# Keys of attention blocks 8 to 23 turned by transposing transfers instead of by PE

## The chip, the cores and the metric

One core of a Trainium2 chip. The time is device microseconds of one execution of the whole program. The kernel before took 1919.92 us (median of two runs, 1918.02 and 1921.83).

## The reference

A chunked attention feeds a mixture of experts. q, k and v are fp32 of shape (4, 8, 768, 64): batch, heads, positions, features.

```python
scale = 1.0 / np.sqrt(D)
for c in range(S // 32):                    # chunks of 32 queries
    k_ctx = k[:, :, max(0, 32*c - 16) : min(S, 32*c + 32 + 8)]
    k_full = concat(mem_k, k_ctx)           # 8 memory keys and a window of up to 56
    scores = scale * q_c @ k_full.T
    a = exp(scores - scores.max(-1)); a /= a.sum(-1) + 1e-9
    out_c = a @ v_full
x = out as (3072, 512)
P = exp(x @ w_gate - max); 8 times: rows of P, then columns, are brought to a common sum
out = sum over 8 experts of P[:, e] * (relu(x @ w1[e]) @ w2[e])     # w1 512x1024, w2 1024x512
```

What the change touches is `q_c @ k_full.T`. To make it on PE, the 64 features must lie on the partitions, so queries and keys are turned (transposed) first. All this is fp32.

## The kernel before, in words

**Two kinds of work.** Attention goes by 24 blocks of 128 queries (6 per batch, each 4 chunks of 32). Four blocks make a unit of 512 tokens; there are 6 units. The expert part goes through 48 steps, one for an expert and a unit, in split fp16 products by a Strassen scheme (`hidden`, `output`: matmuls px, py, pz and yx, yy, yz at line 1598, plain products yp at line 2126 for expert 0). Expert 0 can do a unit only when its four attention blocks are done, so attention blocks and expert 0 are woven together through the first 290 us or so; after that come experts 1 to 7, which need no more attention.

**What sets the order.** Nothing is issued as it is written. Every step is a `Task` with an engine, a cost, a due time and the steps that it waits for; `Plan.run` plays the program through with these costs and writes each engine's instructions in the order that comes out. It is a fixed list per engine, and each engine works through its list in order. Transfers are tasks of SP, with `cost` times 0.5 us for the issuing and `dma` us for the transfer. Where the plan foresees a gap of more than 0.4 us on PE, `Plan.pad` fills it with matmuls on the identity (`warm`, line 427), `int((at - now - 0.1) * 0.8 / 0.11)` of them, whose results nobody uses. Buffers are rings (`Ring`, `buf`): a task that writes a slot waits for the last users of that slot. A block's due time is `needed(n)`: 50 us for four blocks, from 88 us at block 8 on.

**A block.** `load_block` (lines 831 to 851) loads 128 query rows (q) and 128 key rows (k, beginning 16 positions ahead of the block), both as rows of 8 heads x 64 features, 256 bytes a head. `load_extra` (766 to 827) loads for the four blocks of a unit the 24 keys after each block's 128 and 8 memory keys into one tile kx of 4 x 32 rows; PE turns kx (line 806, tx) and ACT copies it to kxT (line 813). `transposed` (995 to 1044) lets PE turn q (line 1006, tq) and k (line 1010, tk), four 128x128 fp32 transposes each, and ACT copies out of PSUM: qT with the factor 1/8 (line 1034), and into kC the 56-key windows of three chunks (1014), the first 32 keys of the fourth (1020), its next 24 from kxT (1023) and, at the first block of a batch, the 8 memory keys (1027). kC (features of a head pair, 4 pairs, 4 chunks, 64 keys) has one buffer in before. `scores` (1047) multiplies (line 1069, sp), DVE takes the maximum and subtracts it, ACT takes the Exp (line 1108). `values` turns the softmax (ta, 1127), multiplies it with v (xp, 1137), DVE divides (1155), and PE turns the result back (xt, 1178). `load_values` brings v in 8 to 10 transfers a block (line 921). `logits` does the gate's products (lp, lq).

**Queues.** SP issues nearly all transfers: q, k, kx, v; the expert weights w1 and w2 (`load`, lines 549 and 551; the m tiles are a first look for the maxima); stores and loads of the partial sums (akeep, lines 2150, 2013, 1847); stores of a unit's split operands (xkeep, 1256) and of later units' raw ones (gkeep, xs). POOL does the sums for the Strassen blocks of weights (602) and of tokens (1290 to 1314), in order, and copies of memory values (913).

## Time and profile before

| | |
|---|---|
| median of the runs | 1919.92 us |
| profiled execution, span | 1917.9 us |
| PE busy | 1903.2 us (99%), clock 1.000 |
| LDWEIGHTS busy (PEld) | 1641.0 us (86%) |
| DVE, ACT, POOL busy | 1436.4, 1033.6, 524.4 us |
| DMA | 254.82 MB, 133 GB/s over the span |
| 0 to 40 us | PE 36.04 us busy, DMA share 0.85 |
| 40 to 80 us | PE 38.17 us busy, DMA share 0.66 |
| 80 to 120 us | PE 38.54 us busy, DMA share 0.81 |
| 160 to 200 us | PE 39.00 us busy, DMA share 0.84 |
| 240 to 280 us | PE 40.00 us busy, DMA share 0.58 |
| 400 to 500 us | PE 98.65 us busy, DMA share 0.37 |

The program does not wait before or after the span for anything that the profile shows, so its time and the run's are taken as one. PE is busy nearly always. The DMA engines and SP's queue are much busier in the first 280 us, where attention is loaded and expert 0 stores its sums, than later. A query of the trace gives for a line its instructions, their time and what their engine waited for; a view by windows gives the busy time of each engine in a stretch.

### The profile page before, as it was taken

The page shows a single profiled execution, that of the slowest core. Times are in us where ns is not written, and L with a number is a line of the kernel's source. Part 1 is how long each engine was busy: PE and PEld are TensorE (multiplying, and loading weights), DVE is VectorE, ACT ScalarE, POOL GpSimd, SP SyncE. Part 2 cuts the span into 40 slices and gives each one's busy share as a digit, 9 for nine tenths or more (in the row PEclk, how much of TensorE's full clock was granted, in tenths as well). Part 3 has the DMA queues.
Part 4 walks back from the last instruction along what each step waited for, and adds up shares of the span by engine and source line. Part 5 has one row for each costly group of instructions (what it writes and reads, how often), then busy time and mean ns, then how long its engine had stood idle before and what let it go on. Part 6 is the DMA issues. An engine that isn't in the chain of part 4 may idle for free.

```text
span 1917.9 us, 47295 instructions
## 1 busy us (share of the span) xinstructions
PE 1903.2 (99%) x19616; PEld 1641.0 (86%) x19616; DVE 1436.4 (75%) x2396; ACT 1033.6 (54%) x2019; POOL 524.4 (27%) x549
## 2 busy tenths in 40 slices
PE   9999999999999999999999999999999999999999
PEld 7777676688888888888888888888888888888888
DVE  6776569778679866898668875898678885786565
ACT  4765565556456545646445554655555554564453
POOL 1220001544224221432124231342124232332112
PEclk9999999999999999999999999999999999999999
DMA  8678753453235342265214533245313732322321
GB/s 198 174 194 209 171 172 116 129 204 125 83 110 172 127 148 85 78 197 185 92 63 149 197 105 127 78 160 176 138 45 105 242 122 94 100 83 84 127 83 67
DMA packets 246791, 254.82 MB, mean 133 GB/s; under 512 B 113264, under 2 KB 180272, under 8 KB 242224
## 3 DMA queue, kind: packets, MB, share of 16 engines
q1 hardware_dynamic: 244452, 251.21, 41.2%
q8 instruction: 153, 2.51, 0.6%
q10 hardware_dynamic: 2124, 0.59, 0.2%
q14 instruction: 62, 0.51, 0.1%
HBM read 187.84 MB, written 63.44 MB: 131 GB/s over the span
## 4 chain that ended last, share of the span: by engine, by line
PE 96%; DMA 2%; DVE 1%; ACT 0%; issue 0%; SPq 0%; ACTq 0%; DVEq 0%
PE px L1598 26%; PE yx L1598 23%; PE pz L1598 13%; PE yz L1598 11%; PE py L1598 6%; PE yp L2126 6%; PE yy L1598 6%; DMA q<-in_q_dram 1%; PE xp L1137 1%; PE sp L1069 1%; PE pp L2045 1%; PE tq L1006 1%; PE tk L1010 0%; PE ta L1127 0%; PE xt L1178 0%; DVE w L521 0%
## 5 line engine op out<-in xcount | busy, mean ns | idle before, releaser
L1598 PEld LDWEIGHTS <-w 128*128 128x128 f16 x7896 | 771.4, 98 | 91.9 <-issue 0.6
L1598 PEld LDWEIGHTS <-h 128*128 128x128 f16 x7056 | 690.4, 98 | 81.4 <-issue 1.5
L1598 PE MATMUL px<-x,w 128*128 128x256 f16 x4512 | 549.1, 273 | 0.0
L1931 POOL TENSOR_TENSOR acc<-acc,y 128x256 f32<-128x256 f32 x252 | 267.5, 1068 | 862.1 <-ACT y L1906 842.7
L1598 PE MATMUL yx<-w,h 128*128 128x256 f16 x4032 | 467.5, 273 | 1.3 <-DVE acc L1941 1.3
L1657 ACT ACTIVATE q<-px 128x256 f32<-128x256 f32 x376 | 142.8, 381 | 294.2 <-PE px L1598 289.5
L1598 PE MATMUL pz<-x,w 128*128 128x256 f16 x2256 | 278.2, 273 | 0.0
L1598 PE MATMUL yz<-w,h 128*128 128x256 f16 x2016 | 233.8, 273 | 0.0
L1826 DVE TENSOR_TENSOR h<-ss,h 128x1024 f16<-128x1024 f32 x160 | 215.0, 1346 | 4.0 <-ACT h L1802 3.5
L1777 ACT ACTIVATE h<-c 128x768 f16<-128x768 f32 x168 | 140.8, 838 | 106.4 <-DVE c L1667 106.4
L1802 ACT CAST h<-ss 128x1024 f16<-128x1024 f32 x168 | 174.1, 1039 | 20.4 <-DVE ss L1766 19.6
L1766 DVE SCALAR_TENSOR_TENSOR ss<-c,ss 128x256 f32<-128x256 f32 x336 | 168.3, 501 | 8.2
L1810 DVE SCALAR_TENSOR_TENSOR h<-c,h 128x768 f16<-128x768 f32 x168 | 165.3, 984 | 9.2 <-ACT h L1777 9.1
L1667 DVE SCALAR_TENSOR_TENSOR c<-px,q 128x256 f32<-128x256 f32 x188 | 78.0, 422 | 103.2 <-PE px L1598 94.9
L1906 ACT ACTIVATE y<-yx,pscale 128x256 f32<-128x256 f32 x168 | 79.4, 473 | 114.8 <-PE yx L1598 110.6
L1598 PE MATMUL py<-x,w 128*128 128x256 f16 x1128 | 139.2, 273 | 0.0
L2126 PE MATMUL yp<-w,h 128*128 128x512 f16 x576 | 132.0, 379 | 0.0
L1667 DVE SCALAR_TENSOR_TENSOR c<-py,q 128x256 f32<-128x256 f32 x188 | 78.5, 422 | 60.2 <-PE py L1598 56.7
L1766 DVE SCALAR_TENSOR_TENSOR ss<-c,h 128x512 f32<-128x512 f32 x168 | 120.8, 719 | 3.1 <-ACT h L1754 3.0
L1598 PE MATMUL yy<-w,h 128*128 128x256 f16 x1008 | 116.9, 273 | 0.0
L2126 PEld LDWEIGHTS <-h 128*128 128x128 f16 x576 | 56.0, 98 | 57.9
L513 ACT ACTIVATE w<-ws,sw 128x1024 f16<-128x1024 f32 (+1 forms) x64 | 69.3, 1089 | 65.5 <-POOL ws L602 65.5
(158 smaller groups left out, 1773.0 us busy)
## 6 DMA issues: line engine op xcount, KB each, us to landing
x<-xkeep SPq DMA_DIRECT2D x28, 1792.0 KB
akeep<-acc SPq DMA_DIRECT2D x168, 256.0 KB
acc<-akeep SPq DMA_DIRECT2D x168, 256.0 KB
w1f<-in_moe_w_dram SPq DMA_DIRECT2D x72, 256.0 KB
w2f<-in_moe_w_dram SPq DMA_DIRECT2D x32, 512.0 KB
w1fm<-in_moe_w_dram SPq DMA_DIRECT2D x56, 256.0 KB
w2fm<-in_moe_w_dram SPq DMA_DIRECT2D x28, 512.0 KB
xkeep<-x SPq DMA_DIRECT2D x6, 1792.0 KB
```

The costliest lines, as they stand in the source:

```text
L513: lambda: nc.scalar.activation(dst(0), src(), AF.Copy, scale=s),
L1598: nc.tensor.matmul(dst.t, a, b, start=(not more and n == 0), stop=(n == end), skip_group_check=more,)
L1657: lambda: nc.scalar.activation(t.t, src.t, AF.Copy, scale=DOWN),
L1667: lambda: nc.vector.scalar_tensor_tensor(c.t[:, o], src.t, DOWN, q.t, op0=ALU.mult, op1=ALU.add),
L1766: lambda: nc.vector.scalar_tensor_tensor(dst(), src(), 0.0, other(), op0=ALU.max, op1=op),
L1777: lambda: nc.scalar.activation(h.t[:, 0, 0:3], c.t, AF.Relu),
L1802: lambda: nc.scalar.copy(h.t[:, 0, 3:7], ss.t),
L1810: lambda: nc.vector.scalar_tensor_tensor(h.t[:, 1, 0:3].rearrange("p a n -> p (a n)"), c.t.rearrange("p a n -> p (a n)"), 0.0, h.t[:, 0, 0 ...
L1826: lambda: spare.tensor_tensor(h.t[:, 1, 3:7], ss.t, h.t[:, 0, 3:7], op=ALU.subtract),
L1906: (lambda: nc.scalar.activation(t.t, src.t, AF.Copy, scale=f))
L1931: lambda: nc.gpsimd.tensor_tensor(acc.t[:, cols], acc.t[:, cols], q.t, op=ALU.add),
L2126: nc.tensor.matmul(py.t, hf.t[:, hl, where[fh], o : o + P], room(fp, WIDE * wl + DM * fh, WIDE * wl + DM * (fh + 1)), start=(fp == 0 and i ...
```

## The change

For blocks 8 to 23 (`DT = 2 * BU = 8`), PE no longer turns the keys, and ACT no longer copies them into kC:

- POOL copies each key tile into a tile of half words: of each fp32 element the two 16-bit halves go to two planes, 128 rows x 2 x 512 (`plane`, one copy a block). The same for kx of units 2 to 5.
- SP writes the two planes to DRAM, 256 KB a tile (`kplane`, `eplane`).
- SP reads them back by transposing transfers on 2-byte elements (`turn_rows`) straight into kC seen as half words. The planes' rows of one key lie next to each other in DRAM, so that the two halves of a turned element land next to each other. A block has three of 112 rows (56 keys), one of 64 and one of 48 rows (`go_own`, `go_next`), and at the first two blocks after a batch has begun four of 16 rows for the memory keys (`go_memory`). At the first of them here POOL copies the memory keys from the other buffer instead.
- kC gets a second buffer (kC2). Until block 8 its space holds kx and kxT, which were tiles of their own.
- Keys of these blocks are loaded 50 us ahead of need, where it was 25; blocks are loaded one block earlier in program order. Their query transposes stay on PE (`turn_q`).
- For all blocks the factor 1/8 moves from the copy of qT into the scale of the Exp.

The order of all engines comes out of the plan anew. By count of instructions: PE 64 key transposes and 16 of kx fewer, 210 warm matmuls more (378, not 168); ACT 55 instructions fewer; POOL 20 plane copies and one copy of memory keys more; SP 20 plane writes and 96 transposing transfers more.

```diff
@@ -12,6 +12,7 @@
...
 I32 = mybir.dt.int32
+U16 = mybir.dt.uint16
 AF = mybir.ActivationFunctionType
...
@@ -333,6 +334,8 @@
...
     gkeep = [dram.tile([P, KT * GT], F32, name=f"gkeep_{g}") for g in range(2 * NU)]
+    kplane = [dram.tile([2 * QB, H * D], U16, name=f"kplane_{n}") for n in range(NBLK)]
+    eplane = [dram.tile([2 * QB, H * D], U16, name=f"eplane_{u}") for u in range(NU)]
     akeep = [dram.tile([P, DM], F32, name=f"akeep_{T}") for T in range(NT)]
...
@@ -740,9 +743,14 @@
...
+    DT = 2 * BU
     state = {}
     extra = {}
+    extra_users = []
     kC_tile = att.tile([P, HP, CB, KW], F32, name="kC")
+    kC2_tile = att.tile([P, HP, CB, KW], F32, name="kC2")
+    kx_tile = kC2_tile.rearrange("p i c k -> p (i c k)")[:, 0 : H * D].rearrange("p (h d) -> p h d", h=H)
+    kxT_tile = kC2_tile.rearrange("p i c k -> p (i c k)")[:, H * D :].rearrange("p (i t) -> p i t", i=HP)
...
@@ -766,9 +774,13 @@
-        kx = buf("kx", att, [P, H, D], F32, f"kx_{u}")
-        kxT = buf("kxT", att, [P, HP, P], F32, f"kxT_{u}")
-        tx = bank("att", [P, HP, P], f"tx_{u}")
+        if u * BU >= DT:
+            kx = buf("k", att, [P, H, D], F32, f"kx_{u}")
+        else:
+            kx = rings["kx"].take(lambda k: kx_tile)
+        if u * BU < DT:
+            kxT = rings["kxT"].take(lambda k: kxT_tile)
+            extra_users.extend([kx, kxT])
         n0 = u * BU
...
@@ -795,11 +807,17 @@
...
                     (),
-                    needed(n0) - 25.0 + 0.15 if u else BLOCKS[0 if soon else 1] + 0.15,
+                    needed(n0) - (EARLIER if n0 >= DT else 25.0) + 0.15 if u else BLOCKS[0 if soon else 1] + 0.15,
                     [kx],
...
             )
+        if n0 >= DT:
+            planes["x", u] = plane(kx, loads, "k", eplane[u], "POOL", needed(n0) - EARLIER + 4.0, P)
+            return
+        tx = bank("att", [P, HP, P], f"tx_{u}")
...
@@ -829,11 +847,45 @@
...
+    planes = {}
+    fresh = [0]
+    EARLIER = 50.0
+    def plane(src, lds, kind, dst, eng, at, m):
+        pl = buf(kind, att, [P, 2, H * D], U16, f"{kind}p_{dst.name}")
+        def go():
+            a = src.t[0:m].rearrange("p h d -> p (h d)").bitcast(U16)
+            a = a.rearrange("p (x w) -> p w x", w=2)
+            if eng == "ACT":
+                nc.scalar.copy(pl.t[0:m], a)
+            else:
+                nc.gpsimd.tensor_copy(pl.t[0:m], a)
+        t = add(eng, 1.05 if eng == "ACT" else 1.3, go, lds, at, [src, pl])
+        return add(
+            "SP",
+            1,
+            lambda: nc.sync.dma_start(
+                dst.rearrange("(p w) x -> p (w x)", w=2),
+                pl.t[0:m].rearrange("p w x -> p (w x)"),
+            ),
+            [t],
+            at + 2.0,
+            [pl],
+            dma=0.8,
+        )
+    def turn_rows(dst, plane_, r0, m):
+        nc.sync.dma_start_transpose(dst, plane_[2 * r0 : 2 * (r0 + m)])
     def load_block(n):
...
         t0 = blk * QB
-        at = needed(n) - 25.0 if n >= BU else BLOCKS[n]
+        at = needed(n) - EARLIER if n >= DT else needed(n) - 25.0 if n >= BU else BLOCKS[n]
         qt = buf("q", att, [P, H, D], F32, f"q_{n}")
...
@@ -848,6 +900,8 @@
...
         lk = add("SP", 2 if blk == 0 else 1, go_k, (), at + 0.1, [kt], dma=1.55)
+        if n >= DT:
+            planes[n] = (None, plane(kt, [lk], "k", kplane[n], "POOL", at + 4.0, P))
         state[n] = (qt, kt, lq, lk)
...
@@ -990,20 +1044,72 @@
...
+    def turned_by_dma(n):
+        b, blk = divmod(n, NB)
+        at = needed(n) - 9.0
+        qT, done = turn_q(n, at)
+        kC = rings["kC"].take(lambda k: kC2_tile if k else kC_tile)
+        if blk == 0:
+            fresh.clear()
+        memory = len(fresh) < 2
+        fresh.append(n)
+        def window(c, r, plane_, r0, m):
+            dst = kC.t[:, :, c, r : r + m].bitcast(U16)
+            turn_rows(dst, plane_, r0, m)
+        def go_own():
+            for c in range(CB - 1):
+                window(c, 0, kplane[n], c * CH, WIN)
+            window(CB - 1, 0, kplane[n], P - CH, CH)
+        def go_next():
+            window(CB - 1, CH, eplane[n // BU], n % BU * KR, KX)
+        def go_memory():
+            for c in range(CB):
+                window(c, WIN, eplane[m // BU], m % BU * KR + KX, NM)
+        m = n - blk
+        done += [
+            add("SP", 5, go_own, [planes[n][1]], at, [kC], dma=1.8),
+            add("SP", 1, go_next, [planes["x", n // BU]], at, [kC], dma=0.3),
+        ]
+        if memory and m < DT:
+            def copy_memory():
+                nc.gpsimd.tensor_copy(kC.t[:, :, :, WIN:KW], kC_tile[:, :, :, WIN:KW])
+            done.append(add("POOL", 0.4, copy_memory, tr[DT - 1][2], at, [kC]))
+        elif memory:
+            done.append(add("SP", 4, go_memory, [planes["x", m // BU]], at, [kC], dma=0.4))
+        tr[n] = (qT, kC, done)
+    def turn_q(n, at):
+        qt, kt, lq, lk = state[n]
+        qT = buf("qT", att, [P, HP, QB], F32, f"qT_{n}")
+        tq = bank("att", [P, HP, QB], f"tq_{n}")
+        def go_q():
+            for i in range(HP):
+                nc.tensor.transpose(tq.t[:, i], flat(qt, i), ident)
+        t = add("PE", 0.5, go_q, [lq], at, [qt, qT], takes=tq)
+        return qT, [
+            add("ACT", 0.6, lambda: nc.scalar.copy(qT.t, tq.t), [t], at, [qT], frees=tq)
+        ]
     def transposed(n):
+        if n >= DT:
+            return turned_by_dma(n)
         qt, kt, lq, lk = state[n]
...
         r0 = n % BU * KR
-        qT = buf("qT", att, [P, HP, QB], F32, f"qT_{n}")
+        qT, done = turn_q(n, at)
         kC = rings["kC"].take(lambda k: kC_tile)
-        tq = bank("att", [P, HP, QB], f"tq_{n}")
         tk = bank("att", [P, HP, P], f"tk_{n}")
-        def go_q():
-            for i in range(HP):
-                nc.tensor.transpose(tq.t[:, i], flat(qt, i), ident)
...
@@ -1026,18 +1132,6 @@
...
-        t = add("PE", 0.5, go_q, [lq], at, [qt, qT], takes=tq)
-        done = [
-            add(
-                "ACT",
-                0.6,
-                lambda: nc.scalar.activation(qT.t, tq.t, AF.Copy, scale=SCALE),
-                [t],
-                at,
-                [qT],
-                frees=tq,
-            )
-        ]
         t = add("PE", 0.5, go_k, [lk], at, [kt, kC], takes=tk)
...
@@ -1105,7 +1199,7 @@
...
         t = add(
-            "ACT", 0.6, lambda: nc.scalar.activation(s.t, s.t, AF.Exp), [t], at + 1, [s]
+            "ACT", 0.6, lambda: nc.scalar.activation(s.t, s.t, AF.Exp, scale=SCALE), [t], at + 1, [s]
         )
...
@@ -1441,6 +1535,7 @@
...
         transposed(0)
+        load_block(2)
         for n in range(NBLK):
...
@@ -1452,10 +1547,17 @@
...
                 load_values(n + 1)
-            if n + 2 < NBLK:
-                load_block(n + 2)
-                if (n + 2) % BU == 0:
-                    load_extra((n + 2) // BU)
+            if n == DT - 2:
+                rings["kC"].after(1, extra_users[-1].users + extra_users[-2].users)
+                rings["kC"].order, rings["kC"].n = [0, 1], 1
+                load_extra(DT // BU)
+                load_block(DT)
+            if n + 3 < NBLK and n != DT - 3:
+                if n + 3 > DT and (n + 3) % BU == 0:
+                    load_extra((n + 3) // BU)
+                load_block(n + 3)
+            if n + 2 < DT and (n + 2) % BU == 0:
+                load_extra((n + 2) // BU)
             if n % BU == 0 and n > 0:
...
         values(*pend.pop(0))
```

## The prediction

> **What bounds the kernel now.** I read the page's first line and its busy shares, then the windows by stage, then the stage that the change touches, on its own queues.
>
> ```profile
> span 1917.9 us, 47295 instructions
> PE 1903.2 (99%) x19616; PEld 1641.0 (86%) x19616; DVE 1436.4 (75%) x2396; ACT 1033.6 (54%) x2019; POOL 524.4 (27%) x549
> PE 96%; DMA 2%; DVE 1%; ACT 0%; issue 0%; SPq 0%; ACTq 0%; DVEq 0%
> ```
>
> PE is busy 99% of the span and holds 96% of the chain that ended last, at full clock throughout. So there are two ways to move the time: change PE's own work, or make PE wait. The change acts from block 8 on, where the first key load of before lies near 80 us and the last value load near 264 us. Windows of that stage (PE, PEld, DVE, ACT, POOL busy, then clock, DMA share, GB/s):
>
> ```profile
> 80.00:270.00 190.00, 185.63 (x3350) 137.24 (x3351) 123.07 (x234) 117.17 (x243) 27.11 (x37) 1.00 0.74 190
> ```
>
> PE idles 4.4 of 190 us here. DVE, ACT and POOL have room. The DMA engines are 74% busy, the highest share of any long stage, and they are what the change loads. The second thing it loads is SP's queue, which issues nearly every transfer. Its timeline (start, us taken, instruction, count):
>
> ```profile
> 79.01 0.45 SPq L848 DMA_DIRECT2D q<-in_q_dram  x1
> ...
> 91.16 0.98 SPq L549 DMA_DIRECT2D w1f<-in_moe_w_dram  x2
> 92.19 0.75 SPq L890 DMA_DIRECT2D v_pair<-in_mem_v_dram  x2
> 92.98 4.32 SPq L921 DMA_DIRECT2D v_pair<-in_v_dram  x8
> 97.34 0.96 SPq L549 DMA_DIRECT2D w1f<-in_moe_w_dram  x2
> 98.40 0.45 SPq L2150 DMA_DIRECT2D akeep<-acc  x1
> 98.94 0.38 SPq L848 DMA_DIRECT2D q<-in_q_dram  x1
> 99.41 1.04 SPq L845 DMA_DIRECT2D k<-in_k_dram  x1
> 100.50 1.98 SPq L898 DMA_DIRECT2D v_pair<-v_pair  x2
> 102.59 4.17 SPq L921 DMA_DIRECT2D v_pair<-in_v_dram  x8
> ...
> 254.85 9.00 SPq L921 DMA_DIRECT2D v_pair<-in_v_dram  x18
> ```
>
> From 91.16 to 106.76 us SP issues 27 transfers without a break: 0.58 us each. From 79.01 to 263.85 us it issues 247 (the first and last rows above): 184.8 us, or 0.75 us each. By that pitch SP is some three quarters full. The rest is mostly waiting for buffers that PE must free:
>
> ```profile
> SPq L921 <- PE xp L1137: 7.8, 5, 4.3
> SPq L845 <- PE pp L2045: 4.4, 1, 4.4
> SPq L921 <- DMA w2fm<-in_moe_w_dram: 4.2, 3, 2.1
> SPq L2150 <- ACT q L1657: 4.0, 2, 3.6
> ```
>
> These four make 20.4 us (us in total, times, longest). PE in turn already waits for a load now and then, 2.4 us in this stage before the query transposes (busy, mean ns | idle before it):
>
> ```profile
> L1006 PE MATMUL tq<-ident,q 128*128 128x128 f32 x64 | 10.1, 280 | 2.4 <-DMA q<-in_q_dram 2.4
> ```
>
> **The change part by part.**
>
> *Removed from PE.* The key transposes of blocks 8 to 23 and of extra tiles 2 to 5. Both as windows of one line, L1010 and then L806 (PE, PEld busy):
>
> ```profile
> 80.00:270.00 190.00, 9.86 (x64) 7.33 (x64) 1.00 0.74 190
> 80.00:270.00 190.00, 2.43 (x16) 1.85 (x16) 1.00 0.74 190
> ```
>
> L1010 takes 9.86 us for 64 transposes and L806 2.43 us for 16. That is **−12.3 us** on the engine that sets the end, and it is all that the change can give: 0.6%.
>
> *Removed from ACT.* The copies into kC, three per block:
>
> ```profile
> L1014 ACT COPY kC<-tk 128x672 f32<-128x672 f32 x17 | 12.2, 718 | 6.3 <-PE tk L1010 6.3
> L1020 ACT COPY kC<-tk 128x128 f32<-128x128 f32 x17 | 4.6, 271 | 0.0
> L1023 ACT COPY kC<-kxT 128x96 f32<-128x96 f32 x16 | 4.4, 272 | 8.7 <-PE sp L1069 8.7
> ```
>
> That is 21 us in sum, but ACT is 62% busy here and off the path, so I count nothing for it. The scale that moves from q's copy to the Exp costs nothing either: one instruction each, as before. On POOL come 20 copies of 1,024 half words per partition. The nearest row is its 128x1040 copy; 20 of them are 21 us on an engine that is busy 27 of 190. Below it stands the longest wait that POOL has in this stage:
>
> ```profile
> L913 POOL COPY x_room<-v_pair 128x1040 f32<-128x1040 f32 x2 | 2.0, 1052 | 0.0
> ...
> L1298 POOL TENSOR_TENSOR xt<-xg 128x256 f32<-128x256 f32 x6 | 4.5, 757 | 48.6 <-ACT xg L1184 37.9 <-DVE h L1725 10.7
> ```
>
> POOL is in order, and some plane copies stand behind the sums of a unit, which wait for that unit's last attention block (37.9 us once, for xg). The keys are loaded 50 us ahead of need, and four blocks take about 46 us (184.8 / 16 x 4), so a late copy is covered. Without that cover SP would hold at the plane's write, and the value loads behind it on SP with it. Key tiles, extra tiles and planes now share the two slots of the ring k, so each load waits for the copy before it. The longest piece of the chain that is a load of this size:
>
> ```profile
> 79.01 10.05 DMA q<-in_q_dram
> ```
>
> 20 times 10.05 + 1.05 us is 222 us, about the length of the stage, and most loads are faster. I count nothing for it.
>
> *Added to PE.* The planner pads a foreseen gap of PE with warm matmuls, and its order for the changed kernel has 210 more of them (378, not 168), 204 of these ahead of the last attention block's output. Their price is from a run of 19 early in before:
>
> ```profile
> 19.97 2.24 PE L427 MATMUL warm<-ident 128*128 128x256 bf16 x19
> ```
>
> 2.24 / 19 = 0.118 us each, so **+24.8 us** of PE time that is spent whether or not there was a gap. Idle time that they replace is at most the 4.4 us found above.
>
> *Moved on PE.* Up to the last block's output the order now has 174 more matmuls of 256 columns (a 512-column one counted as two). By 12 of them in 1.33 us (a piece of the chain, below) that is 19 us of expert work done earlier, which costs nothing in the end, but tells how far attention was put back: 184.8 + 204 x 0.118 + 19 − 12.3 = **216 us** for the stage if nobody waits.
>
> ```profile
> 302.50 1.33 PE px L1598 x12
> ```
>
> *Added to SP.* 20 plane writes and 96 transposing transfers (64 own windows, 16 next rows, 16 memory rows): 116 issues. No such transfer is in the trace. Bounds for one issue: the shortest row, 0.315 us, and the repeating v_pair copy at 0.70.
>
> ```profile
> L921 SPq DMA_DIRECT2D v_pair<-in_v_dram x146: 315/378/1442, 70.1 to 263.5; - x146
> L898 SPq DMA_DIRECT2D v_pair<-v_pair x12: 685/702/1292, 74.1 to 234.7; - x12
> ```
>
> I take the dense pitch of 0.58, because it holds the queue's own push-back and the shape is like the value loads' (many short runs): 67 us. SP then needs 184.8 + 67 − 20 (its own waits for PE go when SP is the late one) = 232 us where the order leaves 216: **+16 us** of PE waiting. With 0.315 it is 201 us, no wait. With 0.70 it is 246 us, +30.
>
> *Added to the DMA engines.* The totals of the stage (80 to 270 us) and of the stage after it (400 to 1900), each the packets and the share of its main queue:
>
> ```profile
> q1 hardware_dynamic: 80193, 35.64, 72.7%
> ...
> q1 hardware_dynamic: 108147, 180.56, 35.4%
> ```
>
> 72.7% of 16 engines over 190 us is 27.6 ns for a packet of 444 bytes; 35.4% over 1500 us is 78.6 ns for 1,670 bytes. The line through both is 9.1 ns + 0.0416 ns per byte. A plane write is 128 packets of 2 KB: 94 ns each, 0.75 us on 16 engines, 15 us for 20. A block's transposes read 448 rows of 1 KB. In 256-byte pieces, as the k and v loads have (64-element fp32 rows), that is 1,792 packets at 19.8 ns: 2.2 us a block, 37 us with the memory rows. 138 + 15 + 37 = 190 us of work in 216 us: 88%, busy but not over. I take no further term from it. A transposing packet could also be much dearer (second rival).
>
> The Trainium skill has two rules here that disagree. "Advanced Engine Details and Errata" (X-Bar Transpose (TRN2)) says that transposing DMAs are as fast as regular ones, 350 to 400 GB/s; an estimate from it is some 20 us for these 7.6 MB, and the sum stays. "VectorE: DVE Perf Modes" (The three transpose paths) speaks against the change: the Trainium skill's table has 1,309 ns there for a 128x128 2-byte transpose by DMA and 390 ns for one on TensorE. TensorE takes 0.154 us (9.86 / 64) for an fp32 one in this trace, so the second figure is not what this kernel pays; no row shows the first. By it a block would be 14 such squares, by estimate 18 us.
>
> **Sum.** 1917.9 − 12.3 + 24.8 + 16 = 1946.4 us by the profiled execution. Its span is 2.0 us below the median of the runs, so **1948 us**: 1.5% slower.
>
> **Where it shows in the order.** On PE, as unit 1's first product (px_1_0) becomes due; ta is a block's transposed softmax, yp unit 0's output. Before:
>
> ```order
> L2126 MATMUL yp_1800<-w_0_3_386,h_3_1284 128x512
> L481 MATMUL sp_x_1975<-most_of,one 128x1
> L1420 MATMUL lq_1981<-ident,lt_1957 128x128
> L1127 MATMUL ta_1984<-ident,s_1953 128x128 x4
> L2126 LDWEIGHTS h_0_804
> ```
>
> and now, with 30 such pairs of LDWEIGHTS and warm matmul in a row until px_1_0:
>
> ```order
> L2228 MATMUL yp_1900<-w_0_3_415,h_3_1311 128x512
> L484 MATMUL sp_x_1983<-most_of,one 128x1
> L1514 MATMUL lq_1985<-ident,lt_1966 128x128
> L430 LDWEIGHTS ident
> L430 MATMUL warm<-ident 128x256
> ```
>
> The block's work that filled this place has moved behind px_1_0. On SP, from the value loads of block 10 on (k, q: a later block's keys and queries; xkeep, akeep: stores). Before:
>
> ```order
> L921 DMA v_pair<-in_v_dram 56x4x64 x8
> L1256 DMA xkeep_117<-x_2005 128x7168
> L845 DMA k_2252<-in_k_dram 128x8x64
> L2150 DMA akeep_137<-acc_3_2138 128x512
> L848 DMA q_2372<-in_q_dram 128x8x64
> ```
>
> Now:
>
> ```order
> L975 DMA v_pair<-in_v_dram 56x4x64 x8
> L882 DMA_TRANSPOSE kC<-kplane_143 128x4x112 x3
> L882 DMA_TRANSPOSE kC<-kplane_143 128x4x64
> L882 DMA_TRANSPOSE kC_189<-kplane_144 128x4x112 x3
> L882 DMA_TRANSPOSE kC_189<-kplane_144 128x4x64
> L882 DMA_TRANSPOSE kC_189<-eplane_160 128x4x48
> L870 DMA kplane_145<-kp_kplane_145_2453 128x1024
> ```
>
> Nine transposes of blocks 9 and 10 stand ahead of block 11's plane; what is queued behind them on SP is that much later. The plane's write waits for POOL's copy, and the loads behind it on SP wait with it.
>
> **The rivals.** *Floor* (10%): SP catches up in its own gaps, PE does not wait, and the warm matmuls swallow the 4.4 us of idle time: 1919.9 − 12.3 + 24.8 − 4.4 = 1928 us. For it: three quarters of SP's time is used, not all. Against: 116 more issues in one stage.
>
> *The transposing transfers are dear* (35%, slower by over 2%): the memory keys' transfers write rows of 16 half words; suppose that all turned data are moved in runs of that size, 32 bytes. At 9.1 + 1.3 = 10.4 ns, a block's 458,752 bytes are 14,336 pieces: 9.3 us on 16 engines, 149 us for 16 blocks. The engines then need 138 + 15 + 149 = 302 us against 216, and PE waits the 86 us: 1919.9 + 12.5 + 86 = 2018 us. It decides from 4.0 us a block on ((216 − 153) / 16), not twice the copying price; over 2% is passed at about 5.6. For it: most packets of the stage are already small, and fill 74%:
>
> ```profile
> DMA packets 80228, 36.15 MB, mean 190 GB/s; under 512 B 69380, under 2 KB 76609, under 8 KB 79681
> ```
>
> Against: the trace has no transposing transfer at all, and its packets of 256 bytes keep to the line.
>
> *Element by element* (3%): each half word a packet of its own at 9.1 ns is 130 us a block and two milliseconds in all. The instruction is a transpose of its own kind in the order, not a strided copy, so I leave this outside the range.
>
> **How the numbers follow.** The forecast has 50%, the floor 10%, dear transposes 35%, element by element 3%, and 2% are left for a gain that I have overlooked. A measurement of this kernel can tell about 2% from no change, that is 38.4 us. The forecast's own range, 1932 to 1962 from the two prices of an issue, lies within it but for its end; forecast and floor give 0.57 for the same. Dear transposes, the last rival and that end give 0.41 slower. Faster by 2% would need more than PE gets back: the 0.02. The range goes from 1924, just under the floor, to 2012, most of the way to the dear case.
>
> **What would show it.** After: warm x378 on PE; L1116 (the former L1010) with 32 transposes, not 96; SP without breaks from 80 us until past 290; PE waiting 10 to 25 us in 80 to 300 us, ended by transposing transfers or loads; a DMA share near 0.88 there; from 400 us on the stages as before, only shifted. Wrong would be: a transposing issue far from 0.6 us on SP, PE waits over 40 us, a DMA share at 1.0, or any gain below 1918 us.

## The result, and the profile after

The changed kernel takes **2038.64 us** (median of two runs, 2036.53 and 2040.75) against 1919.92: 1.061 times as long (interval 1.0595 to 1.0634), 118.7 us more. The forecast was 1948 us in a range of 1924 to 2012. The direction was right, the size was not. Busy and idle times below are from profiled executions, with spans of 2034.7 us here and 1917.9 before: +116.8 us. The two runs of the changed kernel lie 4.2 us apart and each experiment was run once, so a difference of a few us between two kernels says little.

The page's first lines, the clock's row of its 40 slices, and the chain that ended last by engine and by line:

```profile
span 2034.7 us, 47671 instructions
PE 1956.0 (96%) x19746; PEld 1671.3 (82%) x19746; DVE 1442.8 (71%) x2396; ACT 1015.9 (50%) x1965; POOL 545.8 (27%) x570
PEclk9998888989999999999999999999999999999999
PE 86%; SPq 5%; DVE 4%; DMA 3%; issue 1%; ACT 0%; POOL 0%; DVEq 0%; POOLq 0%; ACTq 0%
PE px L1700 23%; PE yx L1700 21%; PE pz L1700 12%; PE yz L1700 11%; PE py L1700 6%; PE yy L1700 5%; SPq L882 4%; PE yp L2228 3%; PE warm L430 1%; DMA kC<-kplane 1%; PE xp L1231 1%; SPq L975 1%; PE sp L1163 1%; DVE ss L1868 1%; DMA kC<-eplane 1%
```

Two things answer to the lines of before. PE held 96% of the chain and now holds 86%; SP's queue held 0% and now holds 5%, 4 of them in one line, L882, the transposing transfers (DVE's share rose from 1% to 4%). And PE is idle for 2034.7 − 1956.0 = 78.7 us instead of 14.7, while its busy time went up by 52.8 us.

The stage in windows (PE, PEld, DVE, ACT, POOL busy, then clock, DMA share, GB/s):

```profile
80.00:160.00 80.00, 73.24 (x998) 52.27 (x995) 45.72 (x73) 37.16 (x71) 22.92 (x28) 0.98 0.77 209
160.00:240.00 80.00, 59.25 (x814) 43.08 (x815) 30.79 (x57) 23.38 (x45) 10.79 (x11) 0.85 0.57 141
240.00:320.00 80.00, 63.86 (x940) 44.71 (x940) 30.89 (x65) 24.02 (x47) 8.00 (x10) 0.87 0.53 140
320.00:400.00 80.00, 64.33 (x996) 43.31 (x996) 28.77 (x56) 24.23 (x46) 8.32 (x9) 0.91 0.63 170
400.00:440.00 40.00, 30.73 (x270) 20.19 (x269) 32.70 (x90) 13.93 (x26) 6.30 (x6) 0.84 0.27 89
```

PE loses a fifth to a quarter of each stretch from 160 us on, no engine is full, and the DMA share falls to 0.53, where 0.88 was forecast. The granted clock, 1.00 in this stage before, is 0.84 to 0.91 in these stretches. What is nearly full is SP's queue: by the trace's records it is issuing in 282.6 of the 312 us from 79 to 391 us, where before it was in 148.7 of the 184.8. Its timeline (start, us taken, instruction, count):

```profile
107.59 5.22 SPq L882 DMA_TRANSPOSE kC<-kplane  x4
112.86 2.82 SPq L882 DMA_TRANSPOSE kC<-eplane  x2
115.78 0.53 SPq L2252 DMA_DIRECT2D akeep<-acc  x1
116.41 0.37 SPq L870 DMA_DIRECT2D kplane<-kp_kplane  x1
...
128.42 6.38 SPq L975 DMA_DIRECT2D v_pair<-in_v_dram  x8
134.93 10.56 SPq L882 DMA_TRANSPOSE kC<-kplane  x8
145.53 2.22 SPq L882 DMA_TRANSPOSE kC<-eplane  x1
...
385.14 6.53 SPq L882 DMA_TRANSPOSE kC<-kplane  x4
```

Four transposing issues take 5.22 us, eight take 10.56. The groups of the tile kC on SP give the price (duration in ns: least, median, most; then first and last start):

```profile
L882 SPq DMA_TRANSPOSE kC<-kplane x64: 1192/1259/2634, 107.6 to 390.4; - x64
L882 SPq DMA_TRANSPOSE kC<-eplane x32: 1132/1222/3937, 112.9 to 377.8; - x32
```

**An issue holds SP for 1.22 to 1.26 us** by the medians; the first row has transfers of 112 and 64 half-word rows, the second of 48 and 16. 64 x 1.259 + 32 x 1.222 = 120 us of SP's time (the 96 durations of the trace, with some long ones, add up to 130.6), where the prediction had 96 x 0.58 = 56. The last one starts at 390.4 us; before, the last value load began at 263.5.

What PE then waits for (us in total, times, longest):

```profile
PE sp L1163 <- DMA kC<-kplane: 24.6, 22, 4.5
PE sp L1163 <- DMA kC<-eplane: 10.8, 7, 5.6
PE warm L430 <- DVE c L1769: 7.4, 1, 7.4
PE cp L1636 <- DVE cs L1608: 6.9, 4, 3.3
```
```profile
PEld sp L1163 <- issue: 27.3, 22, 5.8
PEld sp L1163 <- DMA kC<-kplane: 20.9, 21, 4.7
```

The first two lines are the scores of a block, which wait for their turned keys. (The load of weights waits beside the matmul that it belongs to, so the PEld rows aren't added to PE's.) The third is one single wait for DVE. The fourth is another wait, the routing's (cp after cs), and plays a part below.

### The profile page after: what moved, and what is told of

It reads as the page before. It is cut to its first block, busy times and chain, and to the rows that moved or that the text cites. A ratio compares the mean times of both kernels' runs of the same rounds, so it can differ in the third digit from the quotient of the medians.

```text
span 2034.7 us, 47671 instructions
## 1 busy us (share of the span) xinstructions
PE 1956.0 (96%) x19746; PEld 1671.3 (82%) x19746; DVE 1442.8 (71%) x2396; ACT 1015.9 (50%) x1965; POOL 545.8 (27%) x570
## 4 chain that ended last, share of the span: by engine, by line
PE 86%; SPq 5%; DVE 4%; DMA 3%; issue 1%; ACT 0%; POOL 0%; DVEq 0%; POOLq 0%; ACTq 0%
PE px L1700 23%; PE yx L1700 21%; PE pz L1700 12%; PE yz L1700 11%; PE py L1700 6%; PE yy L1700 5%; SPq L882 4%; PE yp L2228 3%; PE warm L430 1%; DMA kC<-kplane 1%; PE xp L1231 1%; SPq L975 1%; PE sp L1163 1%; DVE ss L1868 1%; DMA kC<-eplane 1%
## 5 line engine op out<-in xcount | busy, mean ns | idle before, releaser
L2228 PE MATMUL yp<-w,h 128*128 128x512 f16 x576 | 136.1, 388 | 0.0
```

The costliest lines, as they stand in the source:

```text
L2228: nc.tensor.matmul(py.t, hf.t[:, hl, where[fh], o : o + P], room(fp, WIDE * wl + DM * fh, WIDE * wl + DM * (fh + 1)), start=(fp == 0 and i ...
```

## The experiments

Theory A: the time that an issue of a transposing transfer holds its queue. Theory B: the turning of the data itself. Theory C: in the first four experiments, that planes, POOL's copies or the order itself hold PE up; in the later ones, that the order was made from a wrong price. A run of the kernel before stood beside each group: 1920.71, 1918.86 and 1917.74 us. Each experiment starts from the changed kernel.

One number turned out to sort them all: the start of the last score matmul (line sp), the end of attention for PE. It stands in the groups of kC; before, after, and without the turns:

```profile
L1069 PE MATMUL sp<-kC,qT x1536: 212/216/241, 12.6 to 275.3; 64*32 64x64 f32 x192
```
```profile
L1163 PE MATMUL sp<-kC,qT x1536: 212/237/313, 13.6 to 393.6; 64*32 64x64 f32 x192
```
```profile
L1163 PE MATMUL sp<-kC,qT x1536: 212/216/242, 13.4 to 314.1; 64*32 64x64 f32 x192
```

| kernel | us | span | last score | span less last score |
|---|---|---|---|---|
| before | 1919.9 | 1917.9 | 275.3 | 1642.6 |
| after | 2038.6 | 2034.7 | 393.6 | 1641.1 |
| turns left out | 1958.7 | 1956.9 | 314.1 | 1642.8 |
| turns of 16 rows | 2031.3 | 2029.5 | 388.3 | 1641.2 |
| two long turns a block | 1961.1 | 1959.3 | 319.5 | 1639.8 |
| no warm matmuls | 2035.3 | 2033.5 | 392.3 | 1641.2 |
| true price in the plan | 2035.9 | 2034.1 | 391.7 | 1642.4 |
| one long turn a block | 1960.1 | 1958.3 | 318.7 | 1639.6 |
| loads only | 1920.2 | 1918.4 | 275.6 | 1642.8 |
| half the blocks | 1969.4 | 1967.5 | 323.1 | 1644.4 |
| plain copies | 1977.9 | 1976.0 | 337.3 | 1638.7 |
| no planes, no turns | 1943.3 | 1941.5 | 293.6 | 1647.9 |
| planned early | 1954.5 | 1952.7 | 312.1 | 1640.6 |
| turns from ACT | 2023.7 | 2021.9 | 375.0 | 1646.9 |

What follows the last score takes 1639 to 1648 us in all fourteen. To within these 9 us, a microsecond by which attention ends later is a microsecond of the whole.

**The turns left out.** The 96 transposing transfers aren't issued; the scores read what is in kC.

```diff
-        nc.sync.dma_start_transpose(dst, plane_[2 * r0 : 2 * (r0 + m)])
+        return
```

> The changed kernel with the 96 transposing transfers left out; POOL's copies, the plane writes and the order's warm matmuls stay, and scores are made with whatever kC holds, so that part of the computation is missing. Theory A (SP pays some 1.25 us for the issue of a transposing transfer, 96 x 1.25 = 120 us in one queue) and theory B (the data of the turned planes are slow to move) both expect what the rest of the change costs: fewer 12.3 us of transposes, 24.8 us more of warm matmuls, 1932 us within 10. Theory C (planes, POOL's copies or the order itself hold PE up) expects over 1980 us.

1958.7 us. The transfers cost 80 us of the 118.7; the rest of the change costs 39, which no theory had foreseen (A and B are 17 us or more too low, C 21 or more too high). PE hardly waits within the stage; the idle time that shows lies behind it, in 320 to 360 us. Windows of this kernel (the first), and of before around the same work (the second):

```profile
320.00:360.00 40.00, 31.38 (x285) 21.16 (x284) 30.13 (x85) 15.60 (x29) 5.18 (x5) 0.88 0.18 57
```
```profile
280.00:320.00 40.00, 39.98 (x364) 27.27 (x362) 31.92 (x85) 17.54 (x35) 5.49 (x5) 1.00 0.28 96
```

In both, DVE does the long chain of sums that routes the last tokens (85 instructions in each). Before, PE had expert 0's work to do meanwhile. Here part of that work has been done already, ahead of attention's end, and PE idles 8.6 us at a clock of 0.88. The wait behind it:

```profile
PE cp L1636 <- DVE cs L1608: 7.6, 4, 3.3
```

**Turns of 16 rows.** Same 96 transfers, same places, but each turns only 16 rows; the rest of the keys is left out.

```diff
-        nc.sync.dma_start_transpose(dst, plane_[2 * r0 : 2 * (r0 + m)])
+        nc.sync.dma_start_transpose(dst[:, :, 0:16], plane_[2 * r0 : 2 * r0 + 16])
```

> The changed kernel with the same 96 transposing transfers, each cut to 16 rows, so that most of the keys are not turned: 25 KB, not 458 KB per block of own keys and next rows together move this way less than a quarter of the bytes. Theory A expects the same time as the changed kernel, 2038 us within 10, and 1.2 us a piece on SP. Theory B expects most of the loss gone: under 1970 us.

2031.3 us: with a small part of the data (82 of 459 KB a block for own and next rows, not the 25 that the expectation has), all but 7 us of the loss is still there.

```profile
L882 SPq DMA_TRANSPOSE kC<-kplane x64: 1105/1222/2207, 107.3 to 385.3; - x64
L882 SPq DMA_TRANSPOSE kC<-eplane x32: 1095/1222/3872, 113.1 to 373.4; - x32
```

The data is not the cost, the issue is. B falls.

**Two long turns a block.** Instead of six or so short transfers a block, two of 208 rows into the same buffer; the windows of the keys aren't put where they belong.

```diff
+            for i in range(2):
+                nc.sync.dma_start_transpose(
+                    wide[:, :, 208 * i : 208 * (i + 1)], kplane[n][48 * i : 48 * i + 208]
+                )
```

> The changed kernel with two transposing transfers of 208 rows a block in place of its five (or nine): 32, not 96, with nine tenths of the rows; the turned keys do not lie where the scores look for them, next rows and memory keys are left out. Theory A expects 64 x 1.25 = 80 us less on SP and a time of 1945 to 1970 us, with 1.25 us a piece on SP although a piece is twice as long. Theory B expects no more than a tenth of the loss back: over 2020 us.

1961.1 us. Nearly as much is turned as in the change (416 of 448 half-word rows a block; next rows and memory keys are left out), and one run of it takes 2.4 us more than no turn at all.

```profile
L1064 SPq DMA_TRANSPOSE kC<-kplane x32: 1225/1280/2413, 106.8 to 314.1; - x32
```

208 rows take 1.28 us on SP. From here on A is hardly in doubt; the question is how far it goes and what the 39 us are.

**No warm matmuls** after the first 60 us of the plan.

```diff
+        if now > 60.0:
+            return
         for banks in self.free.values():
```

> The changed kernel without the planner's warm matmuls after 60 us of its clock: some 218 fewer. My prediction's term (24.8 us of PE time, spent whether or not there is a gap) expects 2014 us. Theory A expects that they fill time in which PE would wait for SP anyhow: 2030 to 2040 us, with the granted clock of the stage no higher than in the changed kernel. If they hold the granted clock up, the time is above 2040 us and the clock in 160 to 400 us is below 0.83.

2035.3 us, 3 us below the changed kernel's median and 1 below its faster run: no clear gain. There are 218 warm matmuls fewer (160, not 378), but PE idles 94.1 us instead of 78.7, and its clock is lower (0.79 in 160 to 240 us, against 0.85). Most of the warm matmuls stood in gaps that PE had anyway.

```profile
160.00:240.00 80.00, 58.32 (x749) 38.70 (x749) 29.92 (x56) 23.39 (x45) 11.41 (x11) 0.79 0.56 141
```

**The true price in the plan.** The planner gets 1.25 us an issue.

```diff
-            add("SP", 5, go_own, [planes[n][1]], at, [kC], dma=1.8),
-            add("SP", 1, go_next, [planes["x", n // BU]], at, [kC], dma=0.3),
+            add("SP", 10, go_own, [planes[n][1]], at, [kC], dma=1.8),
+            add("SP", 2.5, go_next, [planes["x", n // BU]], at, [kC], dma=0.3),
...
-            done.append(add("SP", 4, go_memory, [planes["x", m // BU]], at, [kC], dma=0.4))
+            done.append(add("SP", 10, go_memory, [planes["x", m // BU]], at, [kC], dma=0.4))
```

> The planner is told what a transposing issue really occupies SP for, 1.25 us instead of some 0.6; the 96 transfers and all that they move are the same. If SP's time decides (theory A), telling it changes little: SP still needs 120 us for them, so 2025 to 2045 us; more warm matmuls (696 in its order, not 378) keep the granted clock near 1.0 in 160 to 400 us, and the lost clock turns into warm work. If the order made from a wrong price is the cause (theory C), attention's work is now put where its keys arrive, other work fills the time, and the kernel comes to 1980 us or less.

2035.9 us; C falls. The loss changed its form only: 696 warm matmuls, 56.7 us idle (2034.1 − 1977.4), a mean clock of 0.990 instead of 0.981, and the same end of attention within 2 us. In 160 to 400 us the clock is 0.94 instead of 0.88, short of the "near 1.0" that was expected.

**One long turn a block**, 20 transfers of 256 rows in all, with ACT copying the windows as before and the planner told 1.25 us an issue; everything is computed.

```diff
+            lambda: turn_rows(kT.t.bitcast(U16), kplane[n], 0, P),
...
+        done.append(add("ACT", 0.8, windows, [t], at, [kC, kT]))
+        done.append(add("ACT", 0.27, last, [t], at, [kC, kT]))
```

> One transposing transfer of 256 rows for each block and one for each unit's extra rows (20 instead of 96), into tiles from which ACT copies the windows of the keys as before the change. All results are computed. Theory A: 20 issues of about 1.25 us are 25 us on SP instead of 120; with the 20 plane writes SP is little fuller than without any transposes, so the time is that of the kernel with the transfers left out, 1959 us, within 12. Rival: turning the data itself, not its issue, holds the keys up (4.8 us from issue to landing or more, ACT's copies behind it): 1985 us or more, with PE waiting behind ACT's key copies.

1960.1 us: the keys of blocks 8 to 23 are turned by transfers, all of them, at the price of no turns at all.

```profile
L883 SPq DMA_TRANSPOSE kC<-kplane x16: 1227/1360/3095, 108.0 to 309.7; - x16
```

From 16 rows to 256 an issue goes from 1.22 to 1.36 us. It is the number of instructions that is paid for, and this form needs a fifth of them.

**Loads only**: no block is turned by transfers.

```diff
-    DT = 2 * BU
+    DT = NBLK
```

> All blocks turn their keys on PE as before the change; what is left of the change is the order of the loads (a block's keys and queries asked for one block sooner in the program) and the scale moved from the query's copy into Exp. Both theories A and C: as before, 1920 within 5 us, 168 warm matmuls. If these two edits carry a part of the 38 us that remain without transposes, it comes to 1930 us or more.

1920.2 us, 1.3 above the run of before beside it. The earlier loads and the moved scale cost nothing, as the prediction had it.

**Half the blocks** (16 to 23) turned by transfers.

```diff
-    DT = 2 * BU
+    DT = 4 * BU
```

> Blocks 8 to 15 turn their keys on PE as before the change, blocks 16 to 23 by transposing transfers: half the dose, 48 transfers and 10 planes. Theory A with the loss in proportion to SP's added time: half of 118, so 1979 us. Theory A with a threshold (SP had about a quarter of the stage free, some 45 us, and now gets 48 x 1.25 + 10 x 0.4 = 64 us of new issues): 20 to 30 us over before plus half of the other cost (19), so 1955 to 1970 us. If the cost sits in the first change-over at block 8 (slots, rings), it stays above 2010 us.

1969.4 us: 49.5 over before, 42% of the loss for half the transfers, at the upper end of what the threshold gave and below proportion (1979). This run alone doesn't tell the two forms apart. The runs with the changed kernel's order fit a threshold: 41 us on SP in two long turns cost 2.4 us over none, 60 us of plain copies (below) 19, and 120 us 80.

**Plain copies.** The 96 transfers stay, as ordinary ones of fp32 key values with the same destinations; the turning is left out.

```diff
-        nc.sync.dma_start_transpose(dst, plane_[2 * r0 : 2 * (r0 + m)])
+        src = k[0, 0, 0 : 8 * m].rearrange("r d -> (r d)")
+        nc.sync.dma_start(dst.bitcast(F32), src.rearrange("(p i t) -> p i t", p=P, i=HP))
```

> Each of the 96 transposing transfers becomes an ordinary transfer of fp32 values from the key input, with the same destination, the same place on SP and the same waits; the turned keys are left out (the scores of blocks 8 to 23 are computed from other numbers). Theory A says that the kind of the instruction costs SP, not the number of transfers: 0.4 to 0.7 us an issue, so some 67 us less on SP, and a time near the half dose, 1960 to 1980 us, with the last score 40 to 60 us later than before. Rival: 96 more transfers behind 20 planes hold the keys up whatever their kind: 2015 us or more.

1977.9 us, in A's range; the last score comes 62 us later than before, 2 more than A allowed.

```profile
L883 SPq DMA_DIRECT2D kC<-in_k_dram x96: 546/629/3548, 106.8 to 333.4; - x96
```

An ordinary issue of this shape takes 0.63 us, close to the 0.58 that the prediction took. The transposing kind takes twice that.

**No planes, no turns.** POOL's copies and the planes' writes are left out too.

```diff
+        return add(eng, 0.1, lambda: None, lds, at, [src, pl])
```

> Left out: the transposing transfers, and the copies on POOL and the writes of the planes as well. What is left is the order made for them, with some 14 us more PE work than before ahead of the last score (318 warm matmuls in all, and work of the experts moved forward). If the end of attention sets the end of the kernel, it comes 14 us plus a little idle time later than before: 1933 to 1945 us. If the planes' own pace (two slots of the ring k) carries the loss that is left without transposes: 1925 us or less. If neither matters: 1959 us, as with the transposes left out alone.

1943.3 us, so the planes carry 15.4 of the 39 us. They carry it as work in the order, not as waits: up to the last score PE is busy for 301.3 us with them and 281.9 without, and idle for 12.8 and 11.7. Of the warm matmuls, 370 stand ahead of the last score with them and 275 without. That the planner foresaw the chain from load to copy to write through two slots, and filled it with warm matmuls and expert work, is the likely reason; no run shows it by itself.

**Planned early.** The form with one long turn, with the planner told that planes and turns are cheap and may start 75 us ahead, so that only 11 us of extra work stand ahead of the last score (edits against that form).

```diff
-    EARLIER = 50.0
+    EARLIER = 75.0
...
-        t = add(eng, 1.05 if eng == "ACT" else 1.3, go, lds, at, [src, pl])
+        t = add(eng, 1.05 if eng == "ACT" else 0.3, go, lds, at, [src, pl])
...
-            at - 6.0,
+            at - 15.0,
```

> One long turn for each block as in the run of that name, all results computed, and the planner told that planes and turns cost little and may start 75 us ahead, so that less warm and less moved work stands ahead of the last score (11 us more than before, not 37). If the order alone sets attention's end and the keys come in time: 1931 to 1940 us. Rival: the keys do take the time that the planner is no longer told of, PE waits for ACT's key copies, and the time stays at 1955 us or more.

1954.5 us: 5.6 better than with the honest price, a miss of the expected 1931 to 1940, and half a microsecond under the rival's 1955. What the planner wasn't told came back as idle time and clock, the largest part in one place:

```profile
160.00:200.00 40.00, 30.71 (x582) 22.24 (x580) 14.99 (x37) 15.81 (x36) 8.10 (x10) 0.91 0.72 165
```

The rival's wait is there, 4.6 us for ACT's key copies, and so are 7.3 us once for ACT's Exp; ACT itself waits 22.6 us for turned keys from 80 to 330 us. In the stretch ahead of this one, 120 to 160 us, the DMA share is 1.03: with SP unburdened and the loads moved up, the DMA engines are full there. Whether this delays the keys, no run shows.

It is the best kernel found that turns by transfers, and 1.9% slower than before. None of these beats the kernel before.

**Turns from ACT** instead of SP, with the true price.

```diff
-        nc.sync.dma_start_transpose(dst, plane_[2 * r0 : 2 * (r0 + m)])
+        nc.scalar.dma_start_transpose(dst, plane_[2 * r0 : 2 * (r0 + m)])
...
-            add("SP", 5, go_own, [planes[n][1]], at, [kC], dma=1.8),
-            add("SP", 1, go_next, [planes["x", n // BU]], at, [kC], dma=0.3),
+            add("ACT", 10, go_own, [planes[n][1]], at, [kC], dma=1.8),
+            add("ACT", 2.5, go_next, [planes["x", n // BU]], at, [kC], dma=0.3),
```

> The 96 transposing transfers are issued by ACT, not SP, and the planner is told 1.25 us for each. All results are computed. Theory A taken further (the issuing engine is held for the whole time, whichever it is): ACT has some 96 us of work in a stage of 190 and gets 120 more; 38 us come from the order, and ACT's copies and Exps stand behind the turns, so 1975 to 2030 us, with ACT's own work late. Rival: the 1.25 us belong to SP's queue, and ACT issues in 0.4 us or less: 1955 to 1965 us.

2023.7 us, as A taken further has it, and ACT's own work does come late: PE waits 10.0 us for its copies of the softmax (xp behind at), where the changed kernel has 0.6. The time belongs to the instruction, not to SP:

```profile
L882 ACTq DMA_TRANSPOSE kC<-kplane x64: 1201/1282/3018, 106.7 to 364.3; - x64
L882 ACTq DMA_TRANSPOSE kC<-eplane x32: 1144/1244/2023, 95.1 to 367.0; - x32
```

## Why the prediction failed, step by step

**Right.** The bound: PE's path, with SP as the queue that becomes late; SP nearly without breaks far past 290 us; 32 key transposes left on PE, 378 warm matmuls; the earlier loads and the moved scale at nothing. The price of the turned data on the DMA engines was right as well. From 80 to 520 us the changed kernel's trace has 28,672 packets of 256 bytes more than the one without turns (92,480 and 63,808), four for each of 7,168 rows, and its packets of that size take 108.3 us of 16 engines, not 72.9: 35.4 us, and 1.0 for the memory rows, where 37 was forecast. The share of 0.88 did not come, because the stage took longer.

The Trainium skill, "Advanced Engine Details and Errata" (X-Bar Transpose (TRN2)), calls transposing DMAs as fast as regular ones. For the data these runs agree: packets of 256 bytes take 18.7 ns on the mean with the turned rows among them and 18.3 without (21.0 in the form with one long turn). For the instruction they do not: 1.25 us against 0.63.

**The step that failed first: "I take the dense pitch of 0.58" an issue, bounds 0.315 and 0.70.** Measured: 1.22 to 1.26 us. Both bounds came from ordinary transfers, and the instruction is another kind. The prediction said itself that it is "a transpose of its own kind in the order" and used that only to reject a rival. The plane writes, at less than the price taken, come to 16 x 0.404 + 4 x 0.567 = 8.7 us:

```profile
L870 SPq DMA_DIRECT2D kplane<-kp_kplane x16: 367/404/1794, 100.3 to 372.1; - x16
```
```profile
L870 SPq DMA_DIRECT2D eplane<-kp_eplane x4: 555/567/1353, 89.9 to 317.9; - x4
```

With both, the same working gives SP 184.8 + 8.7 + 119.7 − 20 = 293 us in a stage of 216: 77 us of waiting, not 16. The −20 was misread on the way: of the four waits behind it only two, 12.2 us, are for PE. And SP's pauses did not all go: it still has 29.5 us without issuing in the 312, after 36.1 in the 184.8 of before.

**The second: the 19 us of moved expert work that "costs nothing in the end".** It cost nearly all of itself. In every run the part behind the last score stayed at 1639 to 1648 us, though it had less to do: the routing of the last tokens takes its time on DVE, and the work moved ahead was what PE did meanwhile. The windows up to the last score and behind it, of before and of the kernel without turns, show it (PE busy is the first number after the length):

```profile
0.00:275.30 275.30, 265.14 (x4790) 198.66 (x4793) 183.28 (x338) 168.30 (x337) 38.07 (x54) 1.00 0.73 183
0.00:314.10 314.10, 301.27 (x5028) 221.37 (x5031) 189.05 (x342) 152.93 (x290) 59.34 (x75) 1.00 0.70 187
```
```profile
275.30:1917.90 1642.60, 1638.02 (x14851) 1442.29 (x14834) 1253.08 (x2058) 865.34 (x1683) 486.37 (x495) 1.00 0.37 124
314.10:1956.90 1642.80, 1626.07 (x14743) 1434.72 (x14727) 1254.16 (x2055) 862.72 (x1675) 485.21 (x495) 0.99 0.36 123
```

Ahead of the last score PE has 36.1 us more busy time at the same clock, and 2.7 more idle time. Behind it PE has 12.0 us less busy time and 12.2 more idle time, in the same length. So what the order puts ahead of attention's end counts whole: −12.3 + 24.8 + 19 = 31.5 us. The run without turns measures 39.

**The third: the form of the wait.** It was forecast as idle time of PE. The runs with and without turns have the same count of PE instructions. PE idles 78.7 us in one and 29.6 (1956.9 − 1927.3) in the other: +49. The other 29 us of the 78 between their spans is PE busy time, 1956.0 against 1927.3, at a clock of 0.85 to 0.91 from 160 to 400 us. The trace's records of the clock agree: up to 450 us it is at half for 78.5 us in one and for 17.1 in the other, and half of that difference is 31 us. The mean score matmul shows it, 224 ns before and 247 after (busy, mean ns, and what ended the idle time, kernel before and after):

```profile
L1069 PE MATMUL sp<-kC,qT 64*32 64x64 f32 x1536 | 21.0, 224 | 0.2 <-ACT kC L1027 0.2
```
```profile
L1163 PE MATMUL sp<-kC,qT 64*32 64x64 f32 x1536 | 31.5, 247 | 40.6 <-DMA kC<-kplane 24.6 <-DMA kC<-eplane 10.8 <-issue 5.0
```

As time lost the two are not added to the wait: 77 us were worked out for it, the spans differ by 78, and with the true price in the plan, at a higher clock, attention ends at the same place within 2 us. PE spends the time that SP is late partly idle and partly slow.

The Trainium skill, "TensorE: Matmul & The Clock Gate" (HAM oscillation — how this bites in real kernels), has the rule: gaps of more than some 3.4 us put the clock back. The waits here reach 4.5 to 7.4 us, so a clock of 0.85 to 0.91 fits it. The run without turns doesn't: its longest wait of PE in 320 to 360 us is 3.3 us (the line of cp above), and the clock there is 0.88. Here shorter gaps were enough; no run varies the gap's length alone.

**The warm term.** +24.8 us "whether or not there was a gap" was too strict. Where PE is late for its keys anyway, the warm matmuls only fill the gap: without most of them nothing clear is won, with 696 of them nothing is lost. Where PE isn't late, as in the kernel without turns, they are part of the 36.1 us above and no idle time went for them, so there they count; no run took them out of it.

**The sum again, with the measured prices.** Last score at 275.3 + 31.5, and beyond it 173.5 us (184.8 + 8.7 − 20) plus the time of the turns' issues on SP, less 216, where that is more than nothing:

| kernel | issues on SP | wait | last score worked out | measured |
|---|---|---|---|---|
| turns left out | 0 | 0 | 306.8 | 314.1 |
| two long turns | 32 x 1.28 = 41 | 0 | 306.8 | 319.5 |
| plain copies | 96 x 0.63 = 60 | 18 | 325 | 337.3 |
| 16 rows | 96 x 1.22 = 117 | 75 | 382 | 388.3 |
| after | 120 | 77 | 384 | 393.6 |

With two prices mended, the prediction's own working holds to 6 to 13 us in all five, always short. The medians leave out the long issues. With the trace's durations added up (turns 43.6, 69.0, 127.0 and 130.6 us from the second row down, planes 9 to 12 in all five), the last two rows come out 5 us too late, plain copies 1 too early, and the first two 7 and 9 too early. In the first row the rest isn't the clock, which is 1.00 up to the last score: it is 4.6 us more PE work than the 31.5 worked out, and 2.7 us of idle time.

**The rivals.** The floor fell with the price. "The transposing transfers are dear" came nearest in time (2018 us), but by a mechanism that the 16-row run excludes: its price was on the data, and the DMA engines never passed a share of 0.77 in these stretches. "Element by element" was further off still. A rival that put the same mistrust on the issue was missing, though the signs of being wrong named it: "a transposing issue far from 0.6 us on SP", and PE waits over 40 us, came true.

**Open** stay three things: what makes up the rest of the last table in its other rows; where the 4.6 us of PE work come from that the count of the order missed; and whether a third slot in the ring of key tiles would make the planes free, which wasn't tried.

## What to carry to other kernels

Price a transfer twice: what the DMA engines do for it, and how long its instruction holds the queue that issues it. Where a kind of instruction isn't in the trace, the rows of another kind bound the first price better than the second, and few long instructions are the safe form. And before calling work that moves ahead free, look at what it used to cover: here it covered the routing at the end of attention, and the whole kernel moved with that end.

## What the runs showed of the hardware

By the medians, a transposing transfer from DRAM held its issuing queue for 1.22 us with 16 half-word rows of 512, 1.26 with 64 or 112, 1.28 with 208 and 1.36 with 256, on SP; on ACT it was 1.24 to 1.28. Ordinary transfers to the same places held it for 0.63. A turned row went as four packets of 256 bytes; packets of that size took 18.7 ns on the mean with turned rows among them, 18.3 without. POOL's deinterleaving copy of 1,024 half words per partition took 1.06 us, at the price of the 1,040-element fp32 copy that stood in for it.

```profile
L864 POOL COPY kp_kplane<-k 128x1024 uint16<-128x1024 uint16 x16 | 17.0, 1060 | 163.2 <-DMA k<-in_k_dram 121.6 <-DMA eplane<-kp_eplane 41.5
```
